# Attention block for one new token: the key and value loads issued by GpSimd, one packet per DMA engine, instead of by SyncE

## The chip, the cores and the metric

One NeuronCore of a Trainium2 chip runs the whole program; nothing runs on the other cores. The metric is device time in microseconds (us), the median over runs. Beside the times there is one profiled execution, whose span is counted from the first to the last instruction.

## The reference, cut to what matters

Two tokens (batch 2, one position each, width 512) go through an attention block with a long cache and then through a small MLP. All is float32.

```python
q = (layernorm(x) @ wq)                  # wq 512 x 4096: 32 heads of 128
scores = q . k_cache * 128**-0.5         # k_cache [2, 32, 8192, 128]
o = softmax(scores) . v_cache            # v_cache [2, 32, 8192, 128]
h = x + o @ wo                           # wo 4096 x 512
r = relu(layernorm(h) @ w1 + b1)         # w1 512 x 1792
out = h + (r * r) @ w2 + b2              # w2 1792 x 512
```

The two caches are 512 MB of the 561 MB that are read; every byte is used once.

## The kernel before, in words

**The pairs.** A *pair* is one head of one batch: 64 pairs, numbered 0 to 63. The host lays the keys and values of a pair side by side in `kvd`, 64 KB per partition on 128 partitions, so that one DMA of 8.39 MB brings a pair. On chip there is a ring of three slots of 64 KB per partition (`slots`, cut into `ring[0..2]`, lines 106 and 107). Pair i stands in slot i mod 3.

**What shares the ring.** The weights `wq` (8.39 MB too) are loaded into slot 2 first, since the queries must be computed before any pair can be; pair 2 follows into the same slot once they are. At the end `wo` goes into slot 1 after pair 61, and `w1` and `w2` into slot 2 after pair 62. Pair 63 stands in slot 0.

**Who loads.** SyncE (`sp`) issues all of these loads, by `load` (line 160), one after the other on its one DMA queue: `wq`, pair 0, pair 1 (lines 167 to 170), then for each further pair a wait on the semaphore `FREE` and the load (lines 171 to 180), then `wo` in two parts, `w1` in two, `w2` in four (lines 181 to 192). ScalarE issues one small load (`small`, 13 KB: the token and the biases, line 168) on its own queue. Each slot has a semaphore `LD[t]`, which a load raises by 16 when all its bytes have landed; TensorE waits for it and takes the 16 back (`take`, lines 95 and 96).

**Who frees.** VectorE raises `FREE` once after the queries (line 261), which frees slot 2 from `wq`, and once after each pair (line 316).

**Start.** VectorE waits for `small`, the layer norm goes through VectorE, TensorE and ScalarE (lines 228 to 238), TensorE waits for `wq` (line 243) and multiplies, VectorE transposes, scales (line 258) and copies the first query (line 260, tile `qc`).

**Each pair.** TensorE multiplies keys by the query in two halves (`front`, line 271), VectorE takes maxima (`maxes`, line 279), ScalarE exponentials (`exps`, line 283), and VectorE multiplies the values by them and sums (`product`, line 288), eight instructions a pair.

**End.** The last pair (lines 402 to 425) is interleaved with the merging of the others; TensorE waits for the two parts of `wo` (lines 427 and 435), then for `w1` (line 461) and `w2` (line 483), and SyncE stores the result (line 496). TensorE's and VectorE's instructions are recorded and emitted later, so the profile puts all of them on line 53.

GpSimd fills the identity matrix `ident` (lines 195 to 198) and does nothing else.

Of the kernel before, what the change touches and what calls it, by code (L numbers as in the profile page):

```python
# [6 lines left out]
ALU = mybir.AluOpType  # L7
# [4 lines left out]
P = 128  # L12
# [8 lines left out]
LAST = BH - 1  # L21
ROUNDS = LAST // 3
# [4 lines left out]
W2_PIECES = [8, 4, 1, 1]  # L27
W1_PIECES = [2, 2]
HA = 20
EPS = 1e-5  # L30
SCALE = DH ** -0.5

# [66 lines left out]
def attention_block_kernel(nc, small, kvd, wqd, wod, w1d, w2d, out):  # L99
    p = Program(nc)  # L100
    pe, dve, act, pool, sp = p.pe, p.dve, nc.scalar, nc.gpsimd, nc.sync

    def sbuf(name, *shape):
        return nc.alloc_sbuf_tensor(name, (P, *shape), F32).ap()

    slots = sbuf("slots", 3 * ROW)
    ring = [slots[:, k * ROW : (k + 1) * ROW] for k in range(3)]
# [10 lines left out]
    ident = sbuf("ident", P)  # L118
# [32 lines left out]
    pm = [nc.alloc_psum_tensor(f"pm{k}", (P, 512), F32).ap() for k in range(2)]  # L151

    LD = [p.sem(f"load{k}") for k in range(3)]
    SM, LO = p.sem("small"), p.sem("wo_b")
    LW1 = [p.sem(f"w1_{k}") for k in range(len(W1_PIECES))]
    LW2 = [p.sem(f"w2_{k}") for k in range(len(W2_PIECES))]
    FREE, SCORES, MAXED, EXPED, BUFFER, QUERY = (p.sem(n) for n in ("free", "scores", "maxed", "exped", "buffer", "query"))
    OUT = nc.alloc_semaphore("out")

    def load(tile, src, sem):  # L160
        sp.dma_start(tile, src).then_inc(sem, 16)
# [2 lines left out]
    W2 = ring[2][:, DB * F : DB * F + FB * D].rearrange("p (m c) -> p m c", c=D)  # L164
    WO = ring[1].rearrange("p (h c) -> p h c", c=D)

    load(ring[2], wqd, LD[2])
    act.dma_start(sm, small).then_inc(SM, 16)
    load(ring[0], kvd[0], LD[0])
    load(ring[1], kvd[1], LD[1])  # L170
    with sp.Fori(0, ROUNDS - 1) as r:
        i = r * 3
        for u in range(3):
            t = (2 + u) % 3
            p.take(sp, FREE)
            load(ring[t], kvd[i + (2 + u)], LD[t])
    p.take(sp, FREE)
    load(ring[2], kvd[LAST - 1], LD[2])
    p.take(sp, FREE)
    load(ring[0], kvd[LAST], LD[0])  # L180
    p.take(sp, FREE)
    load(WO[:, :HA], wod[:, :HA], LD[1])
    load(WO[:, HA:], wod[:, HA:], LO)
    p.take(sp, FREE)
    at = 0
    for k, n in enumerate(W1_PIECES):
        load(W1[:, at : at + n], w1d[:, at : at + n], LW1[k])
# [2 lines left out]
    for k, n in enumerate(W2_PIECES):  # L190
# [1 line left out]
        at += n  # L192


    t_id = p.tell("pool", pool.memset(ident, 0.0))
    p.after("pool", t_id)
    t_id = p.tell("pool", pool.affine_select(out=ident, in_=ident, compare_op=ALU.not_equal, fill=1.0, base=0,
                                             pattern=[[-1, P]], channel_multiplier=1))
    dve.memset(ones_d, 1.0 / D)
    dve.memset(eps_t, EPS)  # L200
    dve.memset(zero, 0.0)
# [38 lines left out]


    p.after("pe", tok)
    p.take(pe, LD[2], 16)
    xs = xr.rearrange("p d r b -> p d (r b)")
    toks = []
    for n in range(2):
# [24 lines left out]
    def front(c, slot):  # L271
        p.take(pe, BUFFER)
        for n in range(CS // 512):
            for j in range(NQ):
                c0 = (c * NQ + j) * CS + n * 512
                ins = pe.matmul(s[c][32 * j : 32 * j + 32, n * 512 : (n + 1) * 512], qc, slot[:, c0 : c0 + 512], start=True, stop=True)
        ins.then_inc(SCORES, 1)
# [15 lines left out]
    first = pe.cut()  # L293
    for u in range(3):
        p.take(pe, QUERY)
        p.take(pe, LD[u], 16)
        for c in range(NC):
            front(c, ring[u])
    pairs = pe.cut()
# [32 lines left out]
    def shift(lo, nb):  # L332
        n2 = nb * NC
        tok = p.tell("dve", dve.tensor_tensor(
            nq[:, : NQ * n2].rearrange("p (j c) -> p j c", c=n2), nm[:, None, lo * NC : lo * NC + n2].to_broadcast([P, NQ, n2]),
            ident.rearrange("p (j m) -> p j m", j=NQ)[:, :, :1].to_broadcast([P, NQ, n2]), op=ALU.mult))
        p.after("pe", tok)
        p.after("dve", p.tell("pe", pe.matmul(pm[0][:, : NQ * n2], pick_all, nq[:, : NQ * n2], start=True, stop=True)))
        tok = p.tell("dve", dve.tensor_reduce(gm[:, lo : lo + nb], pm[0][:, : NQ * nb * NC].rearrange(
            "p (j i c) -> p i j c", j=NQ, c=NC), axis=AX.XY, op=ALU.min))  # L340
        p.after("dve", tok)
        tok = p.tell("dve", dve.tensor_tensor(by_pair(wt, lo, nb), gm[:, lo : lo + nb, None].to_broadcast([P, nb, NC]),
                                              by_pair(nm, lo, nb), op=ALU.subtract))
        p.after("act", tok)
        w = wt[:, lo * NC : (lo + nb) * NC]
        return p.tell("act", act.activation(w, w, AF.Exp))
# [9 lines left out]
    def sums(lo, nb, bank, tok):  # L356
        p.after("pe", tok)
        return p.tell("pe", pe.matmul(bank[:, :nb], pick_all, ll[:, lo : lo + nb], start=True, stop=True))
# [29 lines left out]
    def projected(lo, hi):  # L388
        for h in range(lo, hi):
            j = h % NQ  # L390
            ins = pe.matmul(pm[1][32 * j : 32 * j + 32, :], big[:, h * 32 : h * 32 + 32], WO[:, h, :],
                            start=(h < NQ), stop=(h + NQ >= H))
        return ins
# [5 lines left out]

    side = s[2][:, 512:]  # L400
    t_w = shift(0, NG)
    p.take(pe, LD[0], 16)
    front(0, ring[0])
    t_w = weighted(0, NG, t_w)
    t_l = sums(0, NG, pm[1], t_w)
# [18 lines left out]
    p.take(dve, EXPED)  # L424
    ins = last_products(1, range(NH))
    t_v = p.tell("dve", ins)
    p.take(pe, LD[1], 16)
    projected(0, HA)
    t_l = sums(NG, B, side, t_w)
    t_m = p.tell("dve", dve.tensor_tensor(xb, xT, b2T[:, :, None].to_broadcast([P, DB, B]), op=ALU.add))  # L430
# [4 lines left out]
    p.take(pe, LO, 16)  # L435
    projected(HA, HG)
    p.after("pe", t_o)
# [63 lines left out]
                pe.emit(pairs)  # L501
    pe.emit(pe.cut())
    dve.emit(dve.cut())
    nums = sorted(x.num for x in p.sems)
    assert nums == list(range(nums[0], nums[-1] + 1)), nums
    sp.sem_clear(range(nums[0], nums[-1] + 1))
# [29 lines left out]
```

## Time and profile before

| what | value |
|---|---|
| median of 3 runs | 1303.17 us (1303.01 to 1303.39) |
| span of the profiled execution | 1301.8 us; the runs are 1.4 us longer than it |
| data read | 561 MB, 431 GB/s over the span |
| VectorE busy | 761.3 us (58%) |
| TensorE busy | 402.3 us (31%) |
| ScalarE busy | 160.3 us (12%) |
| GpSimd busy | 0.7 us |

How to read the views: the page's second part cuts the span into 40 slices and gives the busy share of each in tenths (9 is 90% or more); DMA there is the mean busy share of the core's 16 DMA engines. The third part counts the packets of each DMA queue: q1 is SyncE's, q10 is ScalarE's. A *packet* is one record of one DMA engine; before, a pair is 128 packets of 64 KB, eight for each engine, and 16 of four bytes that raise the semaphore. In the sixth part the last number of a row is the median time from issue to landing. SPq, PEq, DVEq, ACTq are the instruction streams of the engines as opposed to their datapaths. In a timeline the first number is the start, the second the time up to the end of the group.

### The profile page before, as it was taken

What the parts mean: (1) busy time and instruction counts of PE and PEld (TensorE: products, weight loads), DVE (VectorE), ACT (ScalarE), POOL (GpSimd) and SP (SyncE); (2) the same over time, 40 slices, a digit from 0 to 9 for tenths busy, and PEclk for the clock granted to TensorE, in tenths of its full rate; (3) what the DMA queues carried; (4) which work ended last, traced back from release to release, by engine and by line L of the source; (5) the groups of instructions that cost most, each with busy time, mean ns of one, the idle gap of its engine ahead of it and who ended that gap; (6) DMA issues with size and microseconds to landing.
All of it is one profiled execution on the core that took longest, in us unless ns stands there. A gap on an engine that the chain in (4) does not pass through costs nothing. (4 is left out here: it accounts for less than half of the span.)

```text
span 1301.8 us, 8743 instructions
## 1 busy us (share of the span) xinstructions
PE 402.3 (31%) x2368; PEld 106.1 (8%) x2368; DVE 761.3 (58%) x1266; ACT 160.3 (12%) x268; POOL 0.7 (0%) x6
## 2 busy tenths in 40 slices
PE   1423223323313313313323323322332332332346
PEld 0100000000000000000000000000000000000012
DVE  0464665575575566566466566466557557556564
ACT  0011011011011011111111101101101101101111
POOL 0000000000000000000000000000000000000000
PEclk9766666566666667666656656566656656665658
DMA  9999999999999999999999999999999999999998
GB/s 416 423 447 423 445 423 447 423 443 427 427 441 423 447 423 445 423 447 423 441 429 425 443 423 447 423 445 423 447 423 441 429 425 443 423 447 423 445 416 367
DMA packets 10804, 561.13 MB, mean 431 GB/s; under 512 B 1328, under 2 KB 1456, under 8 KB 1712
## 3 DMA queue, kind: packets, MB, share of 16 engines
q1 hardware_dynamic: 10656, 561.06, 99.7%
q8 instruction: 3, 0.05, 0.0%
q10 hardware_dynamic: 144, 0.01, 0.0%
q14 instruction: 1, 0.01, 0.0%
HBM read 561.00 MB, written 0.07 MB: 431 GB/s over the span
## 5 line engine op out<-in xcount | busy, mean ns | idle before, releaser
L53 PE MATMUL s<-slots,qc 128*32 128x512 f32 x2048 | 368.1, 884 | 848.4 <-PEq L53 848.4
L53 DVE SCALAR_TENSOR_TENSOR slots<-slots,s 128x1024 f32 (+1 forms) x512 | 589.5, 1217 | 1.8 <-DVEq L53 1.0
L53 DVE TENSOR_REDUCE nm<-s 128x1024 f32 (+1 forms) x128 | 156.8, 1225 | 483.8 <-DVEq L53 483.8
L285 ACT ACTIVATE s<-s,nm 128x1024 f32<-128x1024 f32 x128 | 139.3, 1088 | 1078.5 <-ACTq L96 1078.5
L53 PEld LDWEIGHTS s<-slots,qc 128*32 128x32 f32 x2048 | 92.4, 155 | 1123.4 <-issue 1123.3
L53 DVE DVE_READ_ACCUMULATOR slots<-slots,s (+1 forms) x512 | 42.3, 83 | 0.0
L285 ACT ACTIVATION_READ_ACCUMULATOR s<-s,nm (+1 forms) x128 | 24.7, 193 | 0.0
L53 PE MATMUL s<-slots,xr 128*32 128x512 f32 (+1 forms) x96 | 14.5, 759 | 2.7 <-issue 2.7
L53 DVE TENSOR_REDUCE part<-sm 128x2 f32<-128x8 f32 x1 | 0.2, 161 | 20.4 <-DVEq L53 20.4
L53 DVE COPY qc<-qs 128x32 f32 (+1 forms) x64 | 11.0, 172 | 0.0
L53 PE MATMUL pm<-part,ones_d 128*128 128x2 f32 x6 | 1.8, 364 | 25.3 <-DVE part L53 25.3
L53 PE MATMUL pm<-slots,big 128*32 128x512 f32 x64 | 9.5, 749 | 0.0
L53 PE MATMUL pm<-nq,pick_all 128*128 128x496 f32 (+1 forms) x4 | 2.6, 742 | 17.5 <-DVE nq L53 17.5
L53 DVE STREAM_TRANSPOSE big<-s 128x512 f32<-128x512 f32 x2 | 1.4, 717 | 9.2 <-PE s L53 9.2
L53 PEld LDWEIGHTS s<-slots,xr 128*32 128x32 f32 x96 | 3.7, 137 | 10.6 <-issue 10.6
L223 ACT ACT_TABLE_LOAD x1 | 1.3, 1283 | 26.6 <-PE pm L53 26.6
L53 PE MATMUL s<-slots,a 128*2 128x128 f32 x112 | 3.5, 272 | 1.8 <-PEq L53 1.7
L53 PEld LDWEIGHTS pm<-part,ones_d 128*128 128x128 f32 x6 | 1.5, 312 | 26.5 <-DVE part L53 25.4
L53 DVE RECIPROCAL rstd<-rstd 128x2 f32<-128x2 f32 x2 | 0.3, 166 | 4.8 <-ACT rstd L223 4.8
L53 PEld LDWEIGHTS s<-slots,a 128*2 128x2 f32 x112 | 2.7, 84 | 3.3 <-issue 3.3
L53 PEld LDWEIGHTS pm<-slots,big 128*32 128x32 f32 x64 | 2.4, 135 | 5.4 <-issue 5.4
L53 DVE COPY res<-s 128x128 f32<-128x128 f32 x1 | 0.3, 292 | 4.2 <-PE s L53 4.2
(59 smaller groups left out, 24.2 us busy)
## 6 DMA issues: line engine op xcount, KB each, us to landing
slots<-in_wod SPq DMA_DIRECT2D x1, 5120.0 KB, 33.8
slots<-in_w1d SPq DMA_DIRECT2D x2, 1792.0 KB, 27.4
slots<-in_wod SPq DMA_DIRECT2D x1, 3072.0 KB, 40.7
slots<-in_w2d SPq DMA_DIRECT2D x1, 2048.0 KB, 33.8
slots<-in_kvd SPq DMA_DIRECT2D x64, 41.2
slots<-in_w2d SPq DMA_DIRECT2D x1, 1024.0 KB, 35.9
slots<-in_w2d SPq DMA_DIRECT2D x2, 256.0 KB, 36.0
out<-res SPq DMA_DIRECT2D x1, 64.0 KB, 1.6
```

What stands on the lines that cost most here:

```text
L53: ins = getattr(self.engine, op.name)(*op.args, **op.kwargs)
L223: tok = p.tell("act", act.activation(rstd, bank[:, :B], AF.Sqrt, bias=eps_t, scale=1.0))
L285: act.activation(s[c], s[c], AF.Exp, bias=at(nm, pair, NC, c, 1), scale=1.0, accum_out=at(ls, pair, NC, c, 1)).then_inc(EXPED, 1)
```

## The change

The 64 loads of pairs leave SyncE for GpSimd (`pair_load`), with the option `single_packet`, which writes the eight rows that a DMA engine moves of a pair as one packet, not as one packet each. `wq`, `wo`, `w1`, `w2` and the result stay with SyncE. Since the program starts with both, `wq` no longer stands ahead of pairs 0 and 1 in one queue: it is in SyncE's queue and they are in GpSimd's. A load's count is no longer taken back by TensorE: GpSimd raises a second semaphore, `ISSUED`, behind each load, TensorE takes that and waits for `LD[t]` without lowering it, and GpSimd lowers `LD[t]` by an instruction of its own ahead of the slot's next load. `FREE` goes to GpSimd; for the last two slots it passes it on to SyncE as `GONE`.

```diff
-    load(ring[2], wqd, LD[2])
+    def pair_load(t, pair):
+        pool.dma_start(ring[t], kvd[pair], single_packet=SINGLE).then_inc(LD[t], 16)
+        pool.sem_inc(ISSUED, 1)
+
+    load(ring[2], wqd, LQ)
     act.dma_start(sm, small).then_inc(SM, 16)
-    load(ring[0], kvd[0], LD[0])
-    load(ring[1], kvd[1], LD[1])
-    with sp.Fori(0, ROUNDS - 1) as r:
+    pair_load(0, 0)
+    pair_load(1, 1)
+    t_id = p.tell("pool", pool.memset(ident, 0.0))
...
+    p.take(pool, FREE)
+    pair_load(2, 2)
+    with pool.Fori(0, ROUNDS - 1) as r:
         i = r * 3
-        for u in range(3):
-            t = (2 + u) % 3
-            p.take(sp, FREE)
-            load(ring[t], kvd[i + (2 + u)], LD[t])
+        for t in range(3):
+            p.take(pool, FREE)
+            pool.inc_swdge_sem([LD[t]], [16], mode="sub")
+            pair_load(t, i + (3 + t))
...
+    for _ in range(2):
+        p.take(pool, FREE)
+        pool.sem_inc(GONE, 1)
+    p.take(sp, GONE)
+    load(WO[:, :HA], wod[:, :HA], LA)
     load(WO[:, HA:], wod[:, HA:], LO)
-    p.take(sp, FREE)
+    p.take(sp, GONE)
...
-        p.take(pe, LD[u], 16)
+        p.take(pe, ISSUED)
+        pe.wait_ge(LD[u], 16)
```

At the very end GpSimd lowers the three `LD` once more and raises `FREE` for SyncE, which takes it before it clears the semaphores.

How the start moves is seen in the instruction streams. SyncE's first rows before (`in_wqd` is `wq`, `in_kvd` the pairs; ISA is the wait for `FREE`; the loop has three loads):

```order
L161 DMA slots<-in_wqd 128x16384
L161 DMA slots<-in_kvd 128x16384 x2
L171 UNCONDITIONAL_BRANCH
L161 ISA
L161 DMA slots<-in_kvd 128x16384
L161 ISA
L161 DMA slots<-in_kvd 128x16384
```

and GpSimd's rows now, from its first load into the loop:

```order
L170 DMA slots<-in_kvd 128x16384 x2
L177 MEMSET ident 128x128
L179 ISA
L179 AFFINE_SELECT ident<-ident 128x128
L170 DMA slots<-in_kvd 128x16384
L183 UNCONDITIONAL_BRANCH
L187 ISA
L170 ISA
L170 DMA slots<-in_kvd 128x16384
```

The first two pairs head GpSimd's stream and have no `wq` in front of them; in the loop the wait (L187) and the lowering of `LD[t]` (L170 ISA) precede each load. At the end of the program SyncE's rows before are

```order
L161 DMA slots<-in_kvd 128x16384 x2
L161 DMA slots<-in_wod 128x10240
L161 DMA slots<-in_wod 128x6144
L161 DMA slots<-in_w1d 128x3584 x2
L161 DMA slots<-in_w2d 128x4096
```

and all that SyncE has now, from the program's first row, is

```order
L163 DMA slots<-in_wqd 128x16384
L163 DMA slots<-in_wod 128x10240
L163 DMA slots<-in_wod 128x6144
L163 DMA slots<-in_w1d 128x3584 x2
L163 DMA slots<-in_w2d 128x4096
```

The loads of pairs 62 and 63, which stood ahead of `wo` in SyncE's queue, are in the other queue.

More of the change, by code (lines that the diff above doesn't have):

```diff
@@ L29 @@
 HA = 20
+SINGLE = True
 EPS = 1e-5
@@ L153, in attention_block_kernel @@
     LD = [p.sem(f"load{k}") for k in range(3)]
-    SM, LO = p.sem("small"), p.sem("wo_b")
+    SM, LQ, LA, LO = p.sem("small"), p.sem("wq"), p.sem("wo_a"), p.sem("wo_b")
+    ISSUED, GONE = p.sem("issued"), p.sem("gone")
     LW1 = [p.sem(f"w1_{k}") for k in range(len(W1_PIECES))]
@@ L165, in attention_block_kernel @@
     WO = ring[1].rearrange("p (h c) -> p h c", c=D)
-    load(ring[2], wqd, LD[2])
+    def pair_load(t, pair):
+        pool.dma_start(ring[t], kvd[pair], single_packet=SINGLE).then_inc(LD[t], 16)
+        pool.sem_inc(ISSUED, 1)
+    load(ring[2], wqd, LQ)
     act.dma_start(sm, small).then_inc(SM, 16)
-    load(ring[0], kvd[0], LD[0])
-    load(ring[1], kvd[1], LD[1])
-    with sp.Fori(0, ROUNDS - 1) as r:
-        i = r * 3
-        for u in range(3):
-            t = (2 + u) % 3
-            p.take(sp, FREE)
-            load(ring[t], kvd[i + (2 + u)], LD[t])
-    p.take(sp, FREE)
[L178 to L182, printed above, removed]
+    pair_load(0, 0)
+    pair_load(1, 1)
+    t_id = p.tell("pool", pool.memset(ident, 0.0))
+    p.after("pool", t_id)
+    t_id = p.tell("pool", pool.affine_select(out=ident, in_=ident, compare_op=ALU.not_equal, fill=1.0, base=0,
+                                             pattern=[[-1, P]], channel_multiplier=1))
+    p.take(pool, FREE)
+    pair_load(2, 2)
+    with pool.Fori(0, ROUNDS - 1) as r:
+        i = r * 3
+        for t in range(3):
[3 more added lines that the diff above has]
+    p.take(pool, FREE)
+    pool.inc_swdge_sem([LD[0]], [16], mode="sub")
+    pair_load(0, LAST)
+    for _ in range(2):
+        p.take(pool, FREE)
+        pool.sem_inc(GONE, 1)
+    p.take(sp, GONE)
+    load(WO[:, :HA], wod[:, :HA], LA)
     load(WO[:, HA:], wod[:, HA:], LO)
-    p.take(sp, FREE)
+    p.take(sp, GONE)
     at = 0
@@ L192, in attention_block_kernel @@
         at += n
[L195 to L198, printed above, removed]
     dve.memset(ones_d, 1.0 / D)
@@ L242, in attention_block_kernel @@
     p.after("pe", tok)
-    p.take(pe, LD[2], 16)
+    p.take(pe, LQ, 16)
     xs = xr.rearrange("p d r b -> p d (r b)")
@@ L401, in attention_block_kernel @@
     t_w = shift(0, NG)
-    p.take(pe, LD[0], 16)
+    p.take(pe, ISSUED)
+    pe.wait_ge(LD[0], 16)
     front(0, ring[0])
@@ L426, in attention_block_kernel @@
     t_v = p.tell("dve", ins)
-    p.take(pe, LD[1], 16)
+    p.after("pool", t_v)
+    pool.inc_swdge_sem(LD, [16] * 3, mode="sub")
+    pool.sem_inc(FREE, 1)
+    p.take(pe, LA, 16)
     projected(0, HA)
@@ L503, in attention_block_kernel @@
     dve.emit(dve.cut())
+    p.take(sp, FREE)
     nums = sorted(x.num for x in p.sems)
```

## Prediction

> **What bounds the kernel now.** First the page: span, the DMA row of the 40 slices, the queues.
>
> ```profile
> span 1301.8 us, 8743 instructions
> ...
> DMA  9999999999999999999999999999999999999998
> ...
> q1 hardware_dynamic: 10656, 561.06, 99.7%
> q10 hardware_dynamic: 144, 0.01, 0.0%
> ```
>
> SyncE's queue (q1) keeps the 16 DMA engines busy for 99.7% of the span; no compute engine passes 58%. So the time is the bytes over the DMA rate, plus whatever idle time the DMA engines have. Next the steady state alone, the DMA view of 40 to 1221 us, and the rows of SyncE's line that issues the pairs, with their times to landing:
>
> ```profile
> DMA packets 8784, 511.71 MB, mean 433 GB/s; under 512 B 976, under 2 KB 976, under 8 KB 976
> ...
> q1 hardware_dynamic: 8784, 511.71, 100.1%
> ```
>
> ```profile
> L161 SPq DMA_DIRECT2D slots<-in_kvd x64: 332/333/428, 1.2 to 1221.2; - x64
> L161 SPq FUSED_REGOPS  x60: 46/46/74, 39.9 to 1182.9; - x60
> ...
> DMA to landing us min/median/max: 40.2/41.2/61.2
> ```
>
> From the load at 40.0 us to the last at 1221.2 there are 61 steps, 19.36 us each; 8.39 MB in 19.36 us is 433 GB/s, so the steps are pure transfer. A load lands 41.2 us after its issue, which is 2 x 19.36 + 2.5: at the moment of issue two others are ahead of it, one nearly in. **An issue may come about 2.5 + 19.4 = 22 us later before a DMA engine runs dry.** That is the cover for everything that the change does in the loop. Compute is inside it too, by the stretch of one pair:
>
> ```profile
> 1200.00:1219.40 19.40, 5.34 (x32) 1.37 (x32) 12.78 (x22) 2.41 (x4) 0.00 (x0) 0.68 1.00 432
> ```
>
> VectorE (third figure) works 12.8 us of 19.4. Now the start, the one place where the engines of the chip wait on an order of loads. Timeline and DMA issues:
>
> ```profile
> 0.74 0.40 ACTq L168 DMA_DIRECT2D sm<-in_small  x1
> 0.74 0.20 POOL L195 MEMSET ident<- 128x128 f32 x1 [0.29 <-POOLq L529]
> 0.75 0.39 SPq L161 DMA_DIRECT2D slots<-in_wqd  x1
> ...
> 24.43 0.16 DVE L53 TENSOR_REDUCE part<-sm 128x2 f32<-128x8 f32 x1 [20.40 <-DVEq L53]
> ...
> 28.75 9.73 PE L53 MATMUL s<-slots,xr 128*32 128x512 f32 x64 [2.27 <-issue]
> ...
> 39.52 0.18 DVE L53 COPY qc<-qs 128x32 f32<-128x32 f32 x1
> ```
>
> ```profile
> sm<-in_small ACTq DMA_DIRECT2D x1, 13.0 KB, 23.6
> slots<-in_wqd SPq DMA_DIRECT2D x1, 23.4
> ```
>
> `wq` lands at 0.75 + 23.4 = 24.15 us; 15.8 us later (39.9, the first FUSED_REGOPS) SyncE sees slot 2 free and issues pair 2. Pair 1, issued as the third load at 1.6 us, lands 61.2 us later (the maximum), at 62.8. So pairs 0 and 1 cover the 15.8 us of the queries, with 23 us to spare.
>
> The small load is the telling row: 13 KB, issued at the same moment as `wq` on another queue, needs 23.6 us, as long as 8.39 MB. Its 144 packets are nine for each DMA engine, `wq` has eight long ones and a four-byte one for each, and both end together. **A DMA engine with two queues takes a packet from one, then a packet from the other, whatever their sizes.** Had it shared bytes evenly, or served by arrival, `small` (issued first) would have landed at once.
>
> The Trainium skill, "DMA: Bandwidth & Descriptors", section "Queues, rings and completion order", states the same and adds a point that no run here shows yet: an engine drains a whole packet from one row's ring before it switches, however many descriptors the packet has. By that rule eight rows in one packet hold the engine eight times as long; without it the pairs would alternate with `wq` row by row, and the two sums are the forecast and the first rival below.
>
> **The change, part by part.**
>
> *Start.* `wq` is now alone in SyncE's queue, with pairs 0 and 1 in GpSimd's. GpSimd is free at 0.74 us (row of `ident`), as SyncE is. If a pair's eight rows are one packet of 512 KB, an engine needs 19.4 us for it. An engine then does perhaps one or two packets of `wq` (2.4 us each, an eighth of 19.36), pair 0 whole, one packet of `wq`, pair 1 whole, and then the rest of `wq`. The three loads together end when they did, at about 62.8, but `wq` and `small` are now last, not first: 38.6 us later. What follows `wq` in the chain stays as it is (15.8 us), so slot 2 is free at 62.8 + 15.8 = 78.6. Slots 0 and 1 hold pairs that cannot be worked on without a query; no load can be issued. **The DMA engines idle** from about 62 (landing is seen some 0.7 us after the last byte) until the first byte of pair 2. From issue to first byte SyncE's `wq` bounds it: in the DMA view of 0 to 24 us, in slices of 0.6 us,
>
> ```profile
> GB/s 0 0 109 1420 218 0 0 0 1463 219 109 0 1422 109 109 109 1422 109 109 109 1422 109 109 109 1422 109 109 109 1422 109 109 109 1422 109 109 109 1422 109 109 109
> ```
>
> a packet's bytes stand in the slice in which it begins, and the first round of 16 begins in the fourth, at about 2.2 us, 1.4 after the issue. For GpSimd's way there is no row: at the least that is hidden (0), at the most I allow 3 us; I take 1.4, SyncE's. Idle: 78.6 + 1.4 - 62 = **18 us** (17 to 20).
>
> Can that be made up later? No: the steady state is pure transfer. Does it grow? After the restart TensorE and VectorE work off pairs 0 and 1, already landed; one pair alone takes 17.2 us from the first matmul to the last product,
>
> ```profile
> 1185.50 6.48 PE L53 MATMUL s<-slots,qc 128*32 128x512 f32 x32 [13.44 <-PEq L53]
> ...
> 1202.61 0.08 DVE L53 DVE_READ_ACCUMULATOR slots<-slots,s  x1
> ```
>
> and the next 12.8 more. Slots 0 and 1 come free at about 96 and 109, and pair 2 keeps the DMA busy from 80 to 99. It does not grow.
>
> *Loop.* Per pair GpSimd takes `FREE`, lowers `LD[t]`, writes the descriptors, raises `ISSUED`. None of these has a row: between 0 and, if they hid nothing, all of it. Behind them on GpSimd nothing is queued but the next load; who waits is the load, with 22 us of cover, so 0 unless the three together pass 22 us. TensorE's extra take of `ISSUED` was satisfied some 40 us earlier: 0. The cover is thinner only in the first two loads after the restart (3 and 10 us), which I count in the 17 to 20.
>
> The Trainium skill, "SBUF — State Buffer", section "SBUF: two separate sides", speaks against the change: descriptors of GpSimd's loads are written through a port that VectorE's two-port modes lock. No run here shows it; a stall of one VectorE instruction (1.2 us here) would vanish in the same cover, but it would be paid in full at the restart, where the idle time would be 19.2 us instead of 18.
>
> *Packets.* In the loop an engine has 8 packets of data a pair, 512 in all; now 64, so 448 fewer. What does a packet cost beside its bytes? The nearest row is the result's store, whose packets are 512 bytes (DMA view of 1300 to 1301.8 us):
>
> ```profile
> q1 hardware_dynamic: 144, 0.07, 12.7%
> ```
>
> 12.7% of 1.8 us on 16 engines is 3.7 us for 144 packets, 25 ns each. At the loop's 27 GB/s an engine, 512 bytes take 19 ns, so 6 ns or so is fixed. Bounds: 0 (the cost belongs to the row and stays) and 448 x 25 ns = 11 us; by the 6 ns, 2.7 us. I take **-2 us**.
>
> *End.* Before, `wo` stood behind pair 63. Now it is in the other queue when pair 63's packet begins:
>
> ```profile
> 1240.96 0.80 SPq L161 DMA_DIRECT2D slots<-in_wod  x2
> ...
> 1243.56 6.46 PE L53 MATMUL s<-slots,qc 128*32 128x512 f32 x32 [13.45 <-PEq L53]
> ```
>
> Pair 62 lands at about 1243.4, so at 1241 plus 1 us some engines have begun pair 63 and others have not; those do one packet of `wo` (40 KB, 1.5 us) first, and pair 63 lands up to 1.5 us late, at 1264.3. TensorE is at the merging until then:
>
> ```profile
> 1262.06 2.02 PE L53 MATMUL pm<-nq,pick_all 128*128 128x496 f32 x2 [12.04 <-DVE nq L53]
> 1264.01 0.20 PEld L53 LDWEIGHTS s<-slots,qc 128*32 128x32 f32 x8 [1.45 <-issue]
> ...
> 1289.01 2.04 PE L53 MATMUL s<-slots,xr 128*32 128x448 f32 x16 [0.47 <-issue]
> ...
> 1298.19 1.58 PE L53 MATMUL s<-slots,a 128*2 128x128 f32 x48
> ```
>
> so the end moves by 0 to 1.5 us: **+0.5**. The semaphore `GONE` and the last lowering run beside transfers of 19 us and of the MLP: 0.
>
> *Sum.* 1301.8 + 18 - 2 + 0.5 = 1318.3 for the span; the runs stand 1.4 above it: **1319.7 us**.
>
> **The rivals.**
>
> *The packet does not hold the engine* (the change then doesn't do what it says): the pairs' rows alternate with those of `wq`. For it: every record of this trace is one row. Then `wq` takes twice its time and lands 19.4 us later, at 43.6; pair 2 is issued at 59.3, its first byte is at about 60.7, while pair 1 runs to 62: no idle. But at the end pair 63 alternates with the first part of `wo`: 5.2 MB at 433 GB/s is 12.1 us, pair 63 lands at 1274.9, TensorE starts it 11 us later, and from there the chain to the result has little waiting in it (from 1264.0 to 1289.0 it computes; I give back 1.5 us in the first products, 0.5 in `w1`). About +9: 1303.2 + 9 = 1312.
>
> *The first pairs come late to the engines* (the other side: faster). If GpSimd's way from 0.74 us to the first packet takes so long that seven packets of `wq` are in by then (2.2 + 7 x 2.4 = 19 us), `wq` lands first as before, the 15.8 us are covered and only the saving of packets is left: 1303.2 - 2.7 = 1300.5, between 1292 and 1303. Against it: 17 us are some eighty times the 0.2 us that GpSimd's row above takes.
>
> *The issuing engine does not matter.* The Trainium skill, "DMA: Bandwidth & Descriptors", section "Issuing engines are not separate DMA queues", says that DMAs from all engines interleave on the same 16 and that another issuer saves only issue time. As a mechanism here: loads are served by arrival, `wq` stays first, and the time stays at 1303, less up to 2.7. Against it stands the small load, which came first and was served in turn.
>
> *GpSimd's loads run slower*: a gap at each load while an engine fetches what GpSimd wrote. Each 0.1 us a pair is 64 x 0.1 = 6.4 us on top of the forecast, 1326 and more. Before, the rows show no gap (100.1% busy); two loads always stand queued, which speaks for hiding it.
>
> **How the numbers follow.** Forecast 0.62; rows alternate 0.18; late first pairs 0.07; served by arrival 0.05; slower loads 0.08. The forecast's own range is 1310 to 1323 (packets 0 to -11, idle 17 to 20, end 0 to 1.5). With the first rival (1309 to 1315) and the mild half of the last it makes 1308 to 1326, which leaves out the two fast rivals and the other half, 0.16. A measurement tells about 0.2%, 2.6 us, from no change. Faster: half of the late-pairs case and a third of the arrival case, 0.06; within: the rest of both, 0.06; slower 0.88.
>
> **What would show it.** In the profile after: the small load's and `wq`'s times to landing near 61 us (43 in the first rival, 23 in the fast ones); the second and third of the page's 40 slices of DMA (33 to 98 us) below 9, with 18 us idle between them; VectorE's first reading of `small` near 62.5 and its copy of the first query near 78; steps of the loop between 19.2 and 19.36 us; pair 63 not later against pair 62 than 21 us. The prediction is wrong if `wq` lands before pair 1, or if the steps of the loop are longer than 19.4.

## The result and the profile after

The changed kernel takes 1313.51 us (median of 4 runs, 1313.02 to 1313.86) against 1303.28 before: slower by 0.77%, ratio 1.0077 with a 95% interval of 1.0064 to 1.0089. The forecast was 1319.7 in 1308 to 1326. Direction and range held; the mechanism that the forecast rested on did not occur, and the first rival, with 1312, did. By the prediction's own sign it was wrong: `wq` landed before pair 1.

The page of the changed kernel (q0 is GpSimd's queue):

```profile
span 1311.7 us, 8874 instructions
...
DMA  9999999999999999999999999999999999999995
...
q0 software_dynamic: 9216, 536.88, 94.6%
q1 hardware_dynamic: 1440, 24.18, 4.4%
...
slots<-in_kvd POOLq DMA_DIRECT2D x64, 40.6
```

Two things are to be seen. The DMA row has no dip in its second and third slice, where the forecast put 18 us of idle engines; the only slice below 9 is the last. And q0 has 9216 packets, which is 64 times 144: a pair is still 128 packets of 64 KB and 16 that signal. "One packet per DMA engine" is not what the engines did. The start, in the DMA issues and the timeline:

```profile
sm<-in_small ACTq DMA_DIRECT2D x1, 13.0 KB, 42.6
slots<-in_wqd SPq DMA_DIRECT2D x1, 42.5
```

```profile
43.63 0.16 DVE L54 TENSOR_REDUCE part<-sm 128x2 f32<-128x8 f32 x1 [39.47 <-DVEq L54]
...
57.49 0.18 DVE L54 COPY qc<-qs 128x32 f32<-128x32 f32 x1
58.31 0.55 POOL L170 DMA_DIRECT2D slots<-in_kvd  x1 [55.00 <-POOLq L97]
```

`wq` lands 19.1 us later than before (42.5 against 23.4), not 38.6: its rows took turns with the rows of the pairs. Pair 2 is issued at 58.3 us, and pair 1 lands at about 62.8, so of the 23 us between the two 4.5 are left, and they are not quite enough: pair 2 is on TensorE at 82.7 us, before at 82.5. The loop is as fast as before (window 63 to 1241 us; before, the same window moved 434 GB/s):

```profile
63.00:1241.00 1178.00, 348.80 (x1952) 87.36 (x1952) 722.89 (x1177) 148.31 (x247) 32.32 (x61) 0.64 1.00 433
```

and at its end nearly nothing is lost. TensorE's starts on pairs 62 and 63, with SyncE's issue of `wo`, and the last steps:

```profile
1241.14 0.80 SPq L163 DMA_DIRECT2D slots<-in_wod  x2
1243.98 6.09 PE L54 MATMUL s<-slots,qc 128*32 128x512 f32 x32 [13.83 <-PEq L54]
...
1262.11 2.02 PE L54 MATMUL pm<-nq,pick_all 128*128 128x496 f32 x2 [12.04 <-DVE nq L54]
...
1275.47 3.64 PE L54 MATMUL s<-slots,qc 128*32 128x512 f32 x16 [11.34 <-issue]
...
1310.15 0.35 SPq L511 DMA_DIRECT2D out<-res  x1
```

Pair 62 starts 0.4 us later than before (1243.98 against 1243.56). Pair 63 follows after 31.5 us where it followed after 20.5, and TensorE stands 11.3 us without work ahead of it. From there to the store of the result it is 34.7 us, before 36.1. The 1.4 us are in the matmuls with `w1`, before (first fence) and after (0.6 us more ahead of them and 0.6 less behind them cancel):

```profile
1289.01 2.04 PE L53 MATMUL s<-slots,xr 128*32 128x448 f32 x16 [0.47 <-issue]
...
1291.50 2.76 PE L53 MATMUL s<-slots,xr 128*32 128x448 f32 x16
```

```profile
1301.01 1.71 PE L54 MATMUL s<-slots,xr 128*32 128x448 f32 x16 [0.47 <-issue]
...
1302.96 1.71 PE L54 MATMUL s<-slots,xr 128*32 128x448 f32 x16
```

They did not wait for `w1` before either (its second part landed at about 1290.6). The clock granted to TensorE was 0.81 and 0.61 in the first two groups and 1.00 in the last two; why it differed was not tried. 0.4 + 11.0 - 1.4 = 10.0 us, the whole difference of the spans (1311.7 - 1301.8 = 9.9).

### The profile page after: what moved, and what is told of

Read it like the earlier page. It is cut to its first block, busy times and chain, and to the rows that moved or that the text cites. A ratio compares the mean times of both kernels' runs of the same rounds, so it can differ in the third digit from the quotient of the medians.

```text
span 1311.7 us, 8874 instructions
## 1 busy us (share of the span) xinstructions
PE 396.1 (30%) x2368; PEld 104.6 (8%) x2368; DVE 761.4 (58%) x1266; ACT 160.4 (12%) x268; POOL 34.8 (3%) x70
## 2 busy tenths in 40 slices
DMA packets 10804, 561.13 MB, mean 428 GB/s; under 512 B 1328, under 2 KB 1456, under 8 KB 1712
## 3 DMA queue, kind: packets, MB, share of 16 engines
q0 software_dynamic: 9216, 536.88, 94.6%
## 5 line engine op out<-in xcount | busy, mean ns | idle before, releaser
L54 PE MATMUL s<-slots,qc 128*32 128x512 f32 x2048 | 364.1, 874 | 846.4 <-PEq L54 835.1
L170 POOL DMA_DIRECT2D slots<-in_kvd x64 | 34.1, 532 | 1187.1 <-POOLq L97 1186.3
```

Source lines behind the costliest of these rows:

```text
L54: ins = getattr(self.engine, op.name)(*op.args, **op.kwargs)
L170: pool.dma_start(ring[t], kvd[pair], single_packet=SINGLE).then_inc(LD[t], 16)
```

## The experiments

Two questions: is the loss the sharing between pair 63 and `wo`, or the way in which GpSimd loads? And what is the unit in which the queues take turns? All times stand against runs of the kernel before on the same chip, 1303.8 us in these.

**The end in one queue.** GpSimd issues the weights of the end too:

```diff
-    for _ in range(2):
-        p.take(pool, FREE)
-        pool.sem_inc(GONE, 1)
-    p.take(sp, GONE)
-    load(WO[:, :HA], wod[:, :HA], LA)
...
+    p.take(pool, FREE)
+    pool_load(WO[:, :HA], wod[:, :HA], LA)
...
```

> The changed kernel, but the loads of wo, w1 and w2 are issued by GpSimd too, behind pair 63 in the same queue; wq stays with SyncE. Theory (at the end pair 63 and wo share the engines row by row, and that is nearly the whole loss): pair 63 starts on TensorE 20.4 us after pair 62 (31.5 in the changed kernel), and the time is 1303.3 + 0.5 left at the start = 1303.8 us (1303.2 to 1304.5). Rival (GpSimd's way of loading, its handshakes or its descriptors cost the 10 us, wherever wo is): 1312 to 1314.

Measured 1305.42 us, ratio 1.0013 (1.0004 to 1.0022). TensorE's timeline:

```profile
1244.48 6.24 PE L54 MATMUL s<-slots,qc 128*32 128x512 f32 x32 [13.67 <-PEq L54]
...
1264.71 2.95 PE L54 MATMUL s<-slots,qc 128*32 128x512 f32 x16
```

Pair 63 is back at 20.2 us after pair 62, and 8 of the 10 us are gone. 1305.4 is above the 1304.5 that was expected at most. The profiled execution was the slowest of the eleven, with a span 3.2 us above that of the kernel before: 0.9 us is the start (pair 62 is that late, where 0.5 was priced), and 2.5 us lie behind the start of pair 63. There TensorE's two groups with `w1` and the first with `w2` take 2.5, 3.2 and 3.3 us, before 2.0, 2.8 and 1.9, at granted clocks of 0.67, 0.50 and 0.57, before 0.81, 0.61 and 1.00.

**All large loads in one queue.** As above, and GpSimd issues `wq` ahead of pair 0.

> As the one before, and wq is issued by GpSimd too, ahead of pair 0: every large load in one queue as in the kernel before, only the issuer differs. Theory: 1303.3 us within 0.6, wq lands near 24 us. Rival one (GpSimd's loads are slower in the loop): above 1305. Rival two (fewer packets save time in the loop): 1300.5.

Measured 1305.04 us, ratio 1.0009 (1.0000 to 1.0018). In the loop GpSimd's queue moves what SyncE's did:

```profile
DMA packets 8789, 512.04 MB, mean 434 GB/s; under 512 B 976, under 2 KB 976, under 8 KB 976
```

so neither rival's mechanism is there: GpSimd's loads are not slower and no packets are saved. The time is all the same above the expected range, and at the 1305 from which the first rival was to count. The trace puts the excess at the end: pair 62 starts 0.6 us earlier than before, and from the start of pair 63 on it takes 2.4 us longer. The same three groups of matmuls make 2.1 of that, at granted clocks of 0.72, 0.50 and 0.57. The first with `w2` takes 3.3 us instead of 1.9, as the clock has it (1.9 / 0.57 = 3.4); a wait for the second part of `w1` makes 0.5. Why the clock was lower is open. It was low for the first group with `w2` (3.0 us at 0.61) in one of the runs with `small` below too, where GpSimd loads no weight.

**The kernel before with a second queue for `wo`.** No GpSimd load; ScalarE issues `wo`:

```diff
-    load(WO[:, :HA], wod[:, :HA], LD[1])
-    load(WO[:, HA:], wod[:, HA:], LO)
+    sp.sem_inc(GONE, 1)
...
+    p.take(act, GONE)
+    act.dma_start(WO[:, :HA], wod[:, :HA]).then_inc(LD[1], 16)
+    act.dma_start(WO[:, HA:], wod[:, HA:]).then_inc(LO, 16)
```

> The kernel before, no load by GpSimd at all, but the two loads of wo are issued by ScalarE on its queue at the same moment (behind the exponentials of pair 61, when slot 1 is free). Theory: pair 63 shares the engines with wo just the same, TensorE starts it about 31 us after pair 62, time 1303.3 + 9.5 = 1312.8 us (1311 to 1314). Rival (the loss is of GpSimd's queue): 1303.3, pair 63 20.5 us after pair 62.

Measured 1313.32 us, ratio 1.0076 (1.0060 to 1.0091), the changed kernel's loss without the change. Its timeline:

```profile
1240.31 0.34 ACTq L304 DMA_DIRECT2D slots<-in_wod  x1
...
1243.58 5.52 PE L53 MATMUL s<-slots,qc 128*32 128x512 f32 x32 [14.39 <-PEq L53]
...
1275.05 3.43 PE L53 MATMUL s<-slots,qc 128*32 128x512 f32 x16 [11.89 <-PEq L53]
```

31.5 us again. Who issues is irrelevant; that `wo` is in another queue than pair 63 is enough.

**`wo` in rows of 4 KB.** The changed kernel with smaller turns for `wo`:

```diff
-    load(WO[:, :HA], wod[:, :HA], LA)
-    load(WO[:, HA:], wod[:, HA:], LO)
+    sp.dma_start(WO[:, :HA], wod[:, :HA], max_dma_last_dim=4096).then_inc(LA, 16)
+    sp.dma_start(WO[:, HA:], wod[:, HA:], max_dma_last_dim=4096).then_inc(LO, 16)
```

> The changed kernel with one edit: the descriptors of wo are cut to 4 KB (before 40 and 24 KB). Theory (turn by turn, one descriptor of each queue): in the eight turns of pair 63 an engine now does eight times 4 KB of wo, 1.2 us, not 12 us; pair 63 starts on TensorE about 21.5 us after pair 62; wo itself has 112 more descriptors an engine at 6 to 8 ns, 0.8 us; time 1304 to 1306. Rival (the queues share by bytes or by time, or the loss is not of this sharing): 1312 to 1314, pair 63 as late as in the changed kernel.

Measured 1306.56 us, ratio 1.0020 (1.0011 to 1.0029), half a microsecond over the expected range.

```profile
1245.94 6.54 PE L54 MATMUL s<-slots,qc 128*32 128x512 f32 x32 [13.37 <-PEq L54]
...
1266.57 3.05 PE L54 MATMUL s<-slots,qc 128*32 128x512 f32 x16
```

20.6 us: with the two queues as they are, the size of a row alone gives pair 63 the engines. That they take turns row by row can be counted, in the DMA view of 1246 to 1260 us:

```profile
q0 software_dynamic: 80, 5.24, 86.6%
q1 hardware_dynamic: 80, 0.33, 5.7%
```

80 rows of 64 KB and 80 rows of 4 KB. The profiled execution was again the slowest, with a span 4.7 us above that of the kernel before: pair 62 is 2.4 us late, and the groups with `w1` and `w2` take 2.1 us longer, two of them at a granted clock of 0.50.

**Without the option.** `SINGLE = False` in the changed kernel.

> The changed kernel without the option for one packet per DMA engine. Theory (the option has no bearing on rows of 64 KB: the engines turn to the next queue after every row with or without it): 1313.5 us within 0.8, wq lands at 42 to 43 us, pair 63 as late. Rival (the option does something, if not what was forecast, for instance it saves per-row cost in the loop): the step of a pair differs by more than 0.03 us and the time by 2 us or more.

Measured 1315.44 us, ratio 1.0085 (1.0068 to 1.0102), an interval that overlaps the changed kernel's, and 1.1 us above the expected range. The packets are the same:

```profile
q0 software_dynamic: 9216, 536.88, 94.5%
```

`wq` lands after 42.6 us, pair 63 starts 31.5 us after pair 62, and from pair 2 to pair 62 a step is 19.36 us, as with the option. So the rival does not hold, and for rows of 64 KB the option shows no effect. The runs scatter more (1312.4 to 1316.3). In the profiled one pair 63 starts 0.7 us later than in the changed kernel, and one group with `w1` takes 3.1 us instead of 1.7, at a granted clock of 0.52, with all weights landed.

**Short rows on GpSimd, with and without the option.** The kernel before, in which GpSimd issues `small` (one run each).

```diff
-    act.dma_start(sm, small).then_inc(SM, 16)
+    pool.dma_start(sm, small, single_packet=True).then_inc(SM, 16)
...
```

> The kernel before with one edit: the small load (13 KB, eight rows of 104 bytes for each DMA engine) is issued by GpSimd with the option for one packet. Theory A (a packet of several rows holds an engine, and only rows of 64 KB are too long for it): small needs one or two turns between rows of wq, lands 5 to 9 us after its issue. Theory B (an engine turns after every row, whatever the option says): small lands about 23 us after its issue, as on ScalarE's queue. The time is not expected to move (1303.3), since pairs 0 and 1 cover the start.

> The same without the option. If the option matters for short rows: 23 us to landing here against 5 to 9 with it. If GpSimd's descriptors are grouped in any case: 5 to 9 in both. If never: 23 in both.

The rows with the option (first fence) and without:

```profile
q0 software_dynamic: 32, 0.01, 0.0%
...
sm<-in_small POOLq DMA_DIRECT2D x1, 13.0 KB, 10.3
```

```profile
sm<-in_small POOLq DMA_DIRECT2D x1, 13.0 KB, 10.1
```

Time 1304.2 and 1303.5. `small` has 32 packets where ScalarE's queue has 144: 16 of data, one for each engine, and 16 signals. So packets of several rows do exist, they do save turns (10 us to landing, not 23.6), and GpSimd's loads get them with or without the option. 10 us was above the expected 5 to 9: with the option, the packets of data begin between 6 and 9 us, behind `wq`'s second row, and the signals between 9 and 12, behind its third.

**`wq` in rows of 16 KB.** The changed kernel with small turns for `wq`, to bring about the idle time of the forecast:

```diff
-    load(ring[2], wqd, LQ)
+    sp.dma_start(ring[2], wqd, max_dma_last_dim=16384).then_inc(LQ, 16)
```

> The changed kernel with one edit: the descriptors of wq are cut to 16 KB, so that wq gets 16 KB in each turn against 64 KB of a pair. Theory: pairs 0 and 1 are through after 16 turns of 3.0 us, wq and small land near 61 us, slot 2 is free near 76 us, and the DMA engines idle for 15 to 18 us: this is the idle time that the prediction priced, and the time is 1313.5 + 16.5 = 1330 us (1328 to 1332). Rival (the loop makes up for an idle start, or the queues share by bytes): 1313.5.

Measured 1326.85 us, ratio 1.0175 (1.0158 to 1.0192), 13.3 us above the changed kernel.

```profile
slots<-in_wqd SPq DMA_DIRECT2D x1, 8192.0 KB, 62.3
...
sm<-in_small ACTq DMA_DIRECT2D x1, 13.0 KB, 2.5
```

Stretches from 20 us on; the last two figures are the DMA share and GB/s:

```profile
20.00:62.00 42.00, 0.00 (x0) 0.00 (x0) 0.00 (x0) 0.00 (x0) 0.00 (x0) 1.00 0.97 418
62.00:77.00 15.00, 12.04 (x84) 3.52 (x88) 1.81 (x4) 0.00 (x0) 0.55 (x1) 1.00 0.19 62
```

62 GB/s instead of 433 over 15 us is 12.9 us of idle engines, and 418 over 42 us makes 1.5 more. In the profiled executions pair 62 starts 15.0 us later than in the changed kernel; the medians differ by 13.3. The idle time is real and is paid in full. The median is below the expected range (1328 at least). What the expectation had not seen is that `small` got through ahead of the pairs: it landed after 2.5 us, the first row of a pair began at about 5.5, and so the layer norm was done when `wq` came.

**Pairs in rows of 32 KB.** The changed kernel with `max_dma_last_dim=32768` on the pairs, option on.

> The changed kernel with the pairs cut into 32 KB descriptors, 16 for each DMA engine, still with the option for one packet. Theory A (the option makes one packet whatever the size, and only the 64 KB rows escaped it): an engine is held for 512 KB, wq lands near 61 us, and the time is that of the forecast, 1318 to 1322. Theory B (a packet is never more than 64 KB): two descriptors a turn, wq lands at 43, time as the changed kernel, 1313 to 1315. Theory C (no grouping of long rows at all): 32 KB a turn against 64 KB of wq, so wq lands at 32 us; at the end pair 63 needs 16 turns, eight beside 40 KB and eight beside 24 KB of wo, so it lands behind all of wo, 19 us late, 1319 to 1322 with the start undisturbed.

Measured 1324.04 us, ratio 1.0158 (1.0141 to 1.0175).

```profile
q0 software_dynamic: 17408, 536.88, 94.3%
...
slots<-in_wqd SPq DMA_DIRECT2D x1, 33.1
```

```profile
1248.23 5.79 PE L54 MATMUL s<-slots,qc 128*32 128x512 f32 x32 [14.16 <-PEq L54]
...
1286.18 3.64 PE L54 MATMUL s<-slots,qc 128*32 128x512 f32 x16 [18.10 <-issue]
```

Theory C in each item: the packets double, `wq` gains at the start (33.1), pair 63 loses at the end (37.9 us after pair 62, 18.6 more than a transfer). The excess of 2 us over 1322 is of the loop: pair 62 starts at 1248.23, 4.7 us later than in the kernel before, though the start had cover again (slot 2 free at 50.3 us, and pair 2 on TensorE only 0.1 us later than before). Up to there an engine has moved 63 x 8 = 504 more rows, so 9 ns each.

**`wq` by GpSimd in rows of 16 KB, with and without the option.** The kernel before, with only `wq` on GpSimd (one run each):

```diff
-    load(ring[2], wqd, LD[2])
+    pool.dma_start(ring[2], wqd, single_packet=True, max_dma_last_dim=16384).then_inc(LQ, 16)
...
```

> The kernel before, but wq is issued by GpSimd in 16 KB descriptors, 32 for each DMA engine, with the option for one packet; the pairs stay with SyncE (64 KB a turn). Theory A (the option makes one packet of all 32): wq lands near 23 to 26 us although pair 0 competes, records of 512 KB or an unbroken run of 16 KB ones; time 1303 to 1304. Theory B (a packet is at most 64 KB): wq alternates evenly with pair 0 and lands at 43 us; time 1303 to 1306. Theory C (no grouping): 16 KB a turn against 64 KB, wq lands near 62 us and the engines idle: 1316 to 1320.

> The same without the option. Theory A: here wq lands later than with the option (43 or 62 us). Theories B and C: the same landing with and without it.

1318.2 with the option, 1319.6 without. `wq` with the option:

```profile
q0 software_dynamic: 528, 8.39, 1.5%
...
slots<-in_wqd POOLq DMA_DIRECT2D x1, 8192.0 KB, 61.8
```

528 packets are 32 an engine of 16 KB, and a signal each; without the option the landing is 62.1 us. Theory C: nothing is grouped, and a queue with rows of 16 KB beside one with rows of 64 KB gets a fifth of what the engines move (2.13 of 10.45 MB from 20 to 44 us).

## Why the prediction was right and wrong, step by step

*Bound, and cover in the loop: right.* The loop is pure transfer after as before (433 GB/s). GpSimd's issue takes 0.53 us, everything that it does per pair hides in the 22 us, and with all loads in its queue the kernel is within 1.3 us of before, and that is not in the loop.

*Start: wrong, and this is the step that failed.* "If a pair's eight rows are one packet of 512 KB, an engine needs 19.4 us for it." The `if` was taken from the option's name; the rule of turns that the small load had shown was right, but the turn is one record of the trace, and for rows of 16, 32 and 64 KB a record was one row in all runs: from SyncE's queue and from GpSimd's, and at 16 and 64 KB with the option and without. Hence `wq` at 42.5 us instead of 62, as the first rival had it (43.6 us in the span; 0.87 + 42.5 = 43.4 measured), and 0.4 us lost instead of 18. The pricing behind it was sound: with `wq` made last by small rows, the idle time came and was paid (12.9 us; `small` had come early there).

The Trainium skill, "DMA: Bandwidth & Descriptors", section "Queues, rings and completion order", has the engine drain a whole packet before it switches. The packets of `small` on GpSimd's queue, 13 KB over 16 or 832 bytes each, agree (10.1 us against 23.6). The long rows were packets of their own, as the 9216 packets of the changed kernel show, and so the turn was a row.

*Packets: wrong in its premise.* -2 us was for 448 fewer packets an engine; there are none fewer. The fixed cost of a row was of the right size: 6 ns from the store, 9 ns by the run with 32 KB rows. Part of the gap is in the working: 16 of the store's 144 packets carry four bytes and not 512, and with 128 x 19 ns for the bytes 3.7 us leave 8 to 9 ns a packet.

*End: wrong by the same step.* +0.5 was forecast, on the ground that pair 63 goes as a whole; as rows it alternates with `wo`, and TensorE starts it 11 us late, +10 with what is given back. The first rival had this sum too: 12.1 us by transfer, about +9. Its 2 us of give-back came out as 1.4, but by luck: it looked for most of it in the first products, which gave nothing back (3.6 us against 3.1), and it came with the clock in the groups with `w1`.

So the range held because it took in the rival, and the sign because both cases lost time, at opposite ends of the program; for the forecast's own mechanism both are luck. Its own range was also added up too narrowly: its bounds give 1309 to 1325, not 1310 to 1323. The chance of 0.18 for the rival was too low: every record of the trace before was one row, and that was the only evidence on the size of a turn.

*A small miss in the rival:* it left 1.3 us to spare at the start. In fact the cover is used up there. Slot 2 came free between 58.3 and 59.8 us over the runs of this form, as the multiplications of the queries took 8.5 to 9.9 us, and pair 62 was later the later pair 2 was issued: by 0.4, 0.9, 1.1 and 2.4 us for 58.3, 58.8, 59.1 and 59.8. Why the multiplications differ is open; the granted clock was 1.00 in all of them. The rival had also taken SyncE's 1.4 us from issue to first byte for GpSimd. With `wq` in rows of 16 KB, GpSimd's first load needed some 4 us, beside `wq` (1.4 to 5.5), and its third 1 to 2, with the engines idle (75.2 to 76.4). What makes the difference is not shown.

*The other rivals.* Late first pairs: GpSimd's first load was issued at 1.4 us and its first rows began between 6 and 8.5, late, but far from the 19 us that this rival needs. Slower loads: no, 433 GB/s in the loop. Served by arrival: no, `wq` landed after 42.5 us. The Trainium skill's "Issuing engines are not separate DMA queues" ("DMA: Bandwidth & Descriptors") says that another issuer saves only issue time. The runs agree as to bandwidth (433 to 434 GB/s whoever issues), but not for the time: a second queue took away the order of the loads, and that cost 10 us.

No kernel tried here was clearly faster than the kernel before.

## What to carry to other kernels

When a kernel is bound by transfers, one queue is not only a way of issuing but an order: loads moved to a second queue no longer wait for those ahead of them, nor go ahead of those behind. Look for the load that someone waits for at the start and at the end, and work out what it shares the engines with; in these runs, with rows of 4 to 64 KB, two queues took turns row by row, so the share of each was its row's size over the sum of both, and the size of a row was a handle for priority. Read the size of a turn from the packet counts of the trace, not from an option's name. And before a remainder of one or two microseconds is put down to the change, look at the granted clock of the stage: here it moved the end of the program by 2 us.

## What the runs showed of the hardware that was not expected

- The option for one packet had no visible effect at rows of 64 KB, 16 KB or 104 bytes; with 104 bytes GpSimd's load had one data packet for each engine in any case (32 packets in all with the signals, 144 on ScalarE's queue).
- An engine's turn between two queues was one row of up to 64 KB. With rows of 64 against 64, 32 against 64 and 64 against 16 KB (pairs against `wq`), `wq` landed after 42.5, 33.1 and 62.3 us; eight turns of 2.42 + 2.42 us are 38.7, eight of 2.42 + 1.21 are 29.0, with some 4 us to begin and to land; in the third case it was last.
- A row costs about 9 ns beside its bytes (504 more rows an engine, 4.7 us).
- TensorE's granted clock in the groups with `w1` and `w2` was anything from 0.50 to 1.00, and the same 16 matmuls with `w1` took from 1.7 us (1.00) to 3.2 us (0.50). In the five profiled executions in which pair 63 came late and TensorE stood idle for 11 us or more before it, nine of these ten groups took 1.7 us; in the eight others none did, 2.0 us at the least. That the rest brings the clock was not tried.
